# Attention blocks normalised in pairs, their sink columns read from the normalised block

## The chip, the cores and the metric

The kernel runs on one core of one Trainium2 chip. TensorE (PE, with its weight loads as PEld), VectorE (DVE), ScalarE (ACT), GpSimd (POOL) and the DMA queues run side by side and wait for one another by semaphores. The metric is the device time of one execution in microseconds, as the median of several runs.

## What is computed

An attention with sink keys and a sliding window feeds two feed-forward stages. The change touches the attention alone:

```python
keep = is_sink | in_window              # 4 sink keys, window of 128
scores = np.where(keep, scores, -1000000000.0)
scores = scores - np.max(scores, axis=-1, keepdims=True)
a = np.exp(scores)
a = a / (np.sum(a, axis=-1, keepdims=True) + 1e-09)
return np.matmul(a, v).astype(np.float32)
```

Shapes are 2 batches, 8 heads, 768 positions, 64 values per head. Behind it come a soft mixture of 8 experts (8 rounds of normalising the gates) and a gated product of two projections, each multiplied out with an output matrix.

## The kernel before

`fast_attention` works on 8 units (two heads each) of 6 blocks of 128 query rows: G = 48 blocks, block g being block i = g mod 6 of its unit. A block's keys are the 128 of the block before it, 16 sink columns, and its own 128: 272 columns (i = 0 has its own 128 alone). Since the first key block holds the sinks, only blocks with i of 2 or more need the sink columns apart; they are split into a high and a low part (`ak`, three copies of 2 x 16 columns) and multiplied in one fp32r product.

The loop at the end of the function writes one slot for each g, and that is the order of every engine's queue; there is no scheduler behind it (the schedule is manual). In slot g stand, in this order:

1. PE: the transposing of the sink parts of block g - 4 (`turn_sinks`, L851), then `sinks` in two slots of a unit, then the scores of block g (L801), then the products with v (`pv`, L874) of the unit that is six blocks behind.
2. ACT: the exponentials of block g - 1 with their row sums (L819).
3. DVE: `mask_max` of block g (L810: mask, scale and row maximum, for two heads).
4. `normal(g - 1)`: DVE adds the guard to the sums (L827) and takes the reciprocal (L828); POOL multiplies both heads' rows (L831) into `a`, and for i of 2 or more makes the sink parts (L837 the 16 normalised columns, L840 the high part twice, L843 the low part).
5. PE: `turn(g - 4)`, the transposes of that block's `a` (L860, L861), which DVE copies out (L864).
6. ACT: the copy of the sink parts out of PSUM (L852), and in two slots `leave` (L888).
7. One step of `warm`: work for the next stage, spread over the slots. It puts sums (L403, L181, L184, L189, L197) and splits (L162) on POOL, splits on DVE (L162), casts on ACT, and in four of the slots the gates' logits on PE (L293, L301).

Buffers turn: 3 for the exponentials `ex`, the sums `sm` and the maxima `mx`, 4 for `a` and `ak`, 2 for `sw`. Behind the 48 slots come 7 more that drain the attention while the first expert product starts, and then the feed-forward stages (`rest`, L87 above all).

Of the kernel before, what the change touches and what calls it, by code (L numbers as in the profile page):

```python
# [12 lines left out]
FR = mybir.dt.float32r  # L13
# [3 lines left out]
ALU = mybir.AluOpType  # L17
# [6 lines left out]
NB = S // 128  # L24
NSK = 16
KW = 128 + NSK
SW = 128 + KW
# [16 lines left out]
def fused_kernel(  # L44
# [711 lines left out]
    with tc.If(flag > 0) as cond:  # L756
        fast_attention(tc, env)
# [4 lines left out]
def fast_attention(tc, env):  # L762
# [3 lines left out]
    pe, act, dve, pool = nc.tensor, nc.scalar, nc.vector, nc.gpsimd  # L766
# [6 lines left out]
    def open_pool(n, name):  # L773
        return sides[n].enter_context(
            tc.tile_pool(name=name, bufs=1, side=("left", "right")[n], reuse_waits="tile")
        )

    def tiles(pool, name, n, *shape):
        return [pool.tile([128, *shape], F32, name=f"{name}{i}") for i in range(n)]

    last, soon = open_pool(0, "last"), open_pool(1, "soon")
# [1 line left out]
    env["lasting"](last)  # L783
    vs, ast, at = (env[n][0] for n in ("vs", "ast", "at"))
    sos, exs = tiles(soon, "so", 2, 2, SW), tiles(soon, "ex", 3, 2, SW)
    ats, aks, sws = tiles(last, "a", 4, 2, SW), tiles(last, "ak", 4, 3, 2, NSK), tiles(last, "sw", 2, 2, NSK)
    mxs, sms = tiles(last, "mx", 3, 2), tiles(last, "sm", 3, 2)
    G = UN * NB
    warming = env["warm"]()

    raw_s, exps, attn = {}, {}, {}

    def scores(g):
        u, i = divmod(g, NB)
        lo = KW if i == 0 else 0
        ps = [bank[(2 * g + h) % 3] for h in range(2)]
        for h in range(2):
            r = slice(h * 64, (h + 1) * 64)
            kf = kt[u][r].rearrange("p j c -> p (j c)")
            rhs = kf[:, 0:128] if i == 0 else kf[:, (i - 1) * KW:(i - 1) * KW + SW]  # L800
            pe.matmul(  # L801
                out=ps[h][:, lo:SW], lhsT=qt[u][r, i * 128:(i + 1) * 128], rhs=rhs, start=True, stop=True
            )
        mx, so = mxs[g % 3], sos[g % 2]
        raw_s[g] = so, mx, ps, lo

    def mask_max(g):
        so, mx, ps, lo = raw_s[g]
        for h in range(2):
            dve.tensor_tensor_reduce(  # L810
                out=so[:, h, lo:], in0=ps[h][:, lo:SW], in1=mask[:, 2 - min(g % NB, 2), lo:], scale=-0.125,
                scalar=3.0e38, op0=ALU.add, op1=ALU.min, accum_out=mx[:, h:h + 1],
            )

    def exp(g):
        so, mx, _, lo = raw_s.pop(g)
        sm, ex = sms[g % 3], exs[g % 3]
        for h in range(2):
            act.activation(  # L819
                out=ex[:, h, lo:], in_=so[:, h, lo:], func=ACTF.Exp, scale=-1.0, bias=mx[:, h:h + 1],  # L820
                accum_out=sm[:, h:h + 1],
            )
        exps[g] = ex, sm, lo

    def normal(g):
        ex, sm, lo = exps.pop(g)
        dve.tensor_scalar(out=sm, in0=sm, scalar1=1.0e-9, scalar2=None, op0=ALU.add)  # L827
        dve.reciprocal(out=sm, in_=sm)  # L828
        a = ats[g % 4]
        for h in range(2):  # L830
            pool.tensor_scalar(  # L831
                out=a[:, h, lo:], in0=ex[:, h, lo:], scalar1=sm[:, h:h + 1], scalar2=1.0, op0=ALU.mult, op1=ALU.mult
            )
        ak = None
        if g % NB >= 2:
            ak, sw = aks[g % 4], sws[g % 2]
            pool.tensor_tensor(  # L837
                out=sw, in0=ex[:, :, 128:KW], in1=sm.unsqueeze(2).broadcast_to([128, 2, NSK]), op=ALU.mult
            )
            pool.tensor_copy(  # L840
                out=ak[:, 0::2].bitcast(FR), in_=sw.unsqueeze(1).broadcast_to([128, 2, 2, NSK])
            )
            pool.tensor_tensor(out=ak[:, 1], in0=sw, in1=ak[:, 0], op=ALU.subtract)  # L843
        attn[g] = a, ak

    def turn_sinks(g):
        _, ak = attn[g]
        if ak is None:
            return None
        dst = bank[7][0:6 * NSK, 384:512]  # L850
        pe.transpose(out=dst, in_=ak.rearrange("p n h c -> p (n h c)"), identity=ident)  # L851
        return lambda: act.copy(out=ast[0:6 * NSK, g % NB * 128:g % NB * 128 + 128], in_=dst)  # L852

    def turn(g):
        i = g % NB
        a, _ = attn.pop(g)
        ps = bank[3 + g % 2]
        for h in range(2):
            if i:
                pe.transpose(out=ps[:, h * 256:h * 256 + 128], in_=a[:, h, 0:128], identity=ident)  # L860
            pe.transpose(out=ps[:, h * 256 + 128:h * 256 + 256], in_=a[:, h, KW:SW], identity=ident)  # L861
        c0 = 0 if i else 128
        o = i * 256 - 128
        dve.tensor_copy(  # L864
            out=at[:, :, o + c0:o + 256], in_=ps.rearrange("p (h c) -> p h c", h=2)[:, :, c0:256]
        )

    def pv(u, j):
        v = nat[u]
        spans = [(j, min(j + 2, NB))] if j != 2 else [(2, 3), (3, 4)]  # L870
        for a, b in spans:
            c = slice(j * 256 + (a - j) * 128, j * 256 + (b - j) * 128)
            for h in range(2):
                pe.matmul(  # L874
                    out=bank[6 + a // 3][h * 64:(h + 1) * 64, (a % 3) * 128:(a % 3 + b - a) * 128],
                    lhsT=v[:, j, h], rhs=at[:, h, c],
                    start=j == 0 or a == 3 and j == 2, stop=j == 5 or a == 2 and j == 2, skip_group_check=True,
                )

    def sinks(u, half):  # L880
        a, b = (2, 3) if half == 0 else (3, 6)
        dst = bank[6 + half][:, (a % 3) * 128:(a % 3 + b - a) * 128]
        c = slice(a * 128, b * 128)
        pe.matmul(out=dst, lhsT=vs[:, u], rhs=ast[:, c], start=False, stop=False, skip_group_check=True)

    def leave(u, half):
        b, p = divmod(u, H // 2)
        act.copy(out=xt[:, b, p, half * HT:(half + 1) * HT], in_=bank[6 + half][:, 0:HT])  # L888

    LAG_T, LAG_V = 4, 6  # L890
    for g in range(G + LAG_V + 1):
        u, i = divmod(g, NB)
        t = g - LAG_T
        rest = turn_sinks(t) if 0 <= t < G else None
        w, j = divmod(g - LAG_V, NB) if 0 <= g - LAG_V < G else (0, 0)
        if j in (3, 5):
            sinks(w, j // 5)
        if g < G:
            scores(g)
        for n in range(max(j - 1, 0), j + (j == 5)):  # L900
            pv(w, n)
        if 0 <= g - 1 < G:
            exp(g - 1)
        if g < G:
            mask_max(g)
        if g == 0:
            masks()
        if 0 <= g - 1 < G:
            normal(g - 1)
        if 0 <= t < G:  # L910
            turn(t)
        if rest:
            rest()
        if i == 3 and u + 1 < UN:
            copy_sinks(u + 1)
        if j in (3, 5):
            leave(w, j // 5)
        if (g == 1 or i == 5 and u) and u + 2 < UN:
            load_q(sp, u + 2)
            load_k(sp, u + 2)  # L920
            load_v(u + 2)
        if 4 <= g < 8:
            sink_values((g - 4) * (UN // 4))
        if g == G:
            sides[1].close()
            env["take"](open_pool(1, "steps_r"))
        if g in env["WARM"]:
            next(warming)
# [163 lines left out]
```

## Time and profile before

| | |
|---|---|
| median of 3 runs | 1428.04 us (1427.96 to 1428.43) |
| span of the profiled execution | 1426.2 us |
| share of the span, PE / PEld / DVE / ACT / POOL | 99% / 86% / 70% / 41% / 43% |
| DMA, mean | 90 GB/s |

The profile gives the profiled execution by its span, from its first instruction to its last; no other time of that execution is shown, and the median of the runs lies 1.8 us above it, which is what lies around the span. A busy share is an average over the whole span. Matmuls overlap, so a busy PE says little by itself. The attention takes roughly the first 110 us, and there the shares are quite different from the table; the rows below are mostly from that stretch.

### The profile page before, as it was taken

To read this page: it belongs to the slowest core of one execution; us is meant where nothing else is said; L and a number is where in the kernel's file an instruction comes from. 1 tells how busy PE (TensorE), PEld (TensorE's weight loads), DVE (VectorE), ACT (ScalarE), POOL (GpSimd) and SP (SyncE) were. 2 spreads that over 40 slices of the span, in tenths; PEclk is the share of its full clock that TensorE was granted. 3 is DMA by queue.
4 is the path that set the end of the run, shared out by engine and by line. 5 is a ranking of instruction groups with operands and counts; after the bars stand their busy time and mean duration, and the time that the engine had idled before them with its cause. 6 is when DMAs were issued, how large, how long until landed. Compare 5 with 4: busy or idle time off the path is not lost.

```text
span 1426.2 us, 20470 instructions
## 1 busy us (share of the span) xinstructions
PE 1406.6 (99%) x7219; PEld 1229.2 (86%) x7219; DVE 999.8 (70%) x1978; ACT 586.4 (41%) x1327; POOL 607.8 (43%) x729
## 2 busy tenths in 40 slices
PE   8999999999999999999999999999999999999998
PEld 5558889898898998989989889898899888888997
DVE  7986877676776766786766766775665876777763
ACT  5774434333333333443443333333333444444442
POOL 6994434343434343443344433434343434324430
PEclk8999999999999999999999999999999999999999
DMA  6312333233233323322243323332222121223101
GB/s 187 116 49 60 104 104 110 89 111 119 82 111 107 123 89 111 105 73 89 82 127 103 111 89 119 104 90 67 74 59 75 54 73 55 72 66 112 60 30 47
DMA packets 146352, 128.65 MB, mean 90 GB/s; under 512 B 8192, under 2 KB 117120, under 8 KB 146240
## 3 DMA queue, kind: packets, MB, share of 16 engines
q1 hardware_dynamic: 145808, 126.99, 28.8%
q8 instruction: 58, 0.95, 0.3%
q14 instruction: 54, 0.44, 0.1%
q10 hardware_dynamic: 432, 0.26, 0.1%
HBM read 114.38 MB, written 12.58 MB: 89 GB/s over the span
## 4 chain that ended last, share of the span: by engine, by line
PE 90%; DVE 6%; ACT 1%; issue 1%; POOL 1%; DMA 0%; DVEq 0%; POOLq 0%; ACTq 0%
PE bank L87 84%; PE bank L801 2%; PE bank L874 1%; DVE ring L162 1%; DVE flat L162 1%; PE bank L860 1%; DVE hid L162 1%; PE bank L861 1%; ACT hid L530 1%; DVE room L529 1%; DMA small<-in_window 0%; DVE so L810 0%; PE bank L851 0%; PE bank L453 0%; DVE at L864 0%
## 5 line engine op out<-in xcount | busy, mean ns | idle before, releaser
L87 PE MATMUL bank<-flat,ring 128*128 128x384 f32 x3696 | 729.0, 339 | 6.2 <-DVE mid L340 2.6
L87 PE MATMUL bank<-ring,hid 128*128 128x512 f32 x2736 | 710.6, 395 | 0.3 <-ACT hid L530 0.3
L87 PEld LDWEIGHTS bank<-flat,ring 128*128 128x128 f32 x3696 | 657.3, 188 | 53.6 <-ACT acc L457 3.2
L87 PEld LDWEIGHTS bank<-ring,hid 128*128 128x128 f32 x2736 | 506.3, 188 | 83.9 <-DVE hid L162 2.7
L162 POOL TENSOR_TENSOR ring<-raw,ring 128x512 fp32r<-128x512 f32 x152 | 206.3, 1361 | 383.6 <-ACT ring L194 342.2
L324 ACT ACTIVATE hid<-mid 128x384 fp32r<-128x384 f32 x191 | 100.7, 527 | 420.4 <-DVE mid L344 316.7
L181 POOL TENSOR_TENSOR room<-raw 128x256 f32<-128x256 f32 x88 | 91.5, 1040 | 358.5 <-DVE ring L162 291.8
L325 DVE SCALAR_TENSOR_TENSOR hid<-mid,hid 128x384 fp32r<-128x384 f32 x191 | 127.4, 667 | 43.6 <-ACT hid L324 35.4
L162 DVE TENSOR_TENSOR ring<-raw,ring 128x512 fp32r<-128x512 f32 (+1 forms) x176 | 142.1, 808 | 0.2 <-ACT ring L182 0.2
L342 DVE TENSOR_TENSOR mid<-mid,bank 128x384 f32<-128x384 f32 x87 | 48.1, 553 | 111.3 <-PE bank L87 111.0
L162 DVE TENSOR_TENSOR ring<-room,ring 128x512 fp32r<-128x512 f32 x176 | 116.0, 693 | 0.9 <-ACT ring L211 0.9
L336 ACT COPY mid<-bank 128x384 f32<-128x384 f32 x87 | 41.7, 479 | 142.6 <-PE bank L87 142.3
L340 DVE TENSOR_TENSOR mid<-mid,bank 128x384 f32<-128x384 f32 x87 | 48.0, 552 | 74.6 <-PE bank L87 74.6
L197 POOL TENSOR_TENSOR room<-raw,room 128x256 f32<-128x256 f32 x88 | 83.4, 948 | 6.8
L189 POOL TENSOR_TENSOR room<-room,raw 128x256 f32<-128x256 f32 x88 | 76.5, 869 | 0.0
L184 POOL TENSOR_TENSOR room<-raw 128x256 f32<-128x256 f32 x88 | 69.3, 788 | 13.3 <-DVE ring L162 11.5
L344 DVE TENSOR_TENSOR mid<-mid,bank 128x384 f32<-128x384 f32 x88 | 48.7, 553 | 32.7 <-PE bank L87 31.9
L325 DVE SCALAR_TENSOR_TENSOR hid<-bank,hid 128x384 fp32r<-128x384 f32 x64 | 35.4, 553 | 43.6 <-ACT hid L324 43.6
L351 DVE TENSOR_TENSOR mid<-mid,bank 128x384 f32<-128x384 f32 x88 | 48.4, 550 | 21.2 <-PE bank L87 21.0
L324 ACT ACTIVATE hid<-bank 128x384 fp32r<-128x384 f32 x64 | 31.4, 491 | 58.4 <-PE bank L87 57.0
L205 ACT CAST ring<-room 128x512 fp32r<-128x512 f32 x88 | 54.6, 621 | 2.0 <-POOL room L189 2.0
L211 ACT CAST ring<-room 128x512 fp32r<-128x512 f32 x88 | 54.6, 620 | 0.6 <-POOL room L197 0.3
(154 smaller groups left out, 1194.1 us busy)
## 6 DMA issues: line engine op xcount, KB each, us to landing
raw<-in_moe_w SPq DMA_DIRECT2D x256, 256.0 KB, 2.7
raw<-kept SPq DMA_DIRECT2D x72, 256.0 KB, 3.2
kept<-room SPq DMA_DIRECT2D x36, 256.0 KB, 2.9
raw<-in_moe_w_a SPq DMA_DIRECT2D x12, 512.0 KB, 3.8
raw<-in_moe_w_b SPq DMA_DIRECT2D x12, 512.0 KB, 3.8
raw<-in_moe_w_out SPq DMA_DIRECT2D x12, 512.0 KB, 3.7
out_x<-xt SPq DMA_DIRECT2D x11, 256.0 KB, 2.1
qt<-in_q SPq DMA_DIRECT2D x6, 384.0 KB, 3.1
```

What stands on the lines that cost most here:

```text
L87: pe.matmul(out=dst, lhsT=a, rhs=b, start=start and n == 0, stop=stop and n == 2, skip_group_check=not check,)
L162: eng.tensor_tensor(out=lo, in0=src, in1=hi.bitcast(F32), op=ALU.subtract)
L181: pool.tensor_tensor(out=s1, in0=a21, in1=a22, op=ALU.add)
L184: pool.tensor_tensor(out=s3, in0=a11, in1=a21, op=ALU.subtract)
L189: pool.tensor_tensor(out=s2, in0=s1, in1=a11, op=ALU.subtract)
L197: pool.tensor_tensor(out=s4, in0=a12, in1=s2, op=ALU.subtract)
L205: act.copy(out=halves[0][0], in_=halves[0][2])
L211: act.copy(out=halves[1][0], in_=halves[1][2])
L324: act.activation(out=h[:, 0, f, t0], in_=src, func=ACTF.Relu)
L325: later.append(lambda: dve.scalar_tensor_tensor(out=h[:, 1, f, t0], in0=src, scalar=0.0, in1=h[:, 0, f, t0].bitcast(F32), op0=ALU.max, op1 ...
L344: dve.tensor_tensor(out=m[:, 2], in0=m[:, 1], in1=ps, op=ALU.add)
L351: dve.tensor_tensor(out=m[:, 1], in0=m[:, 1], in1=ps, op=ALU.subtract)
```

## The change

`normal` is called in even slots only, and does two blocks, g - 2 and g - 1, at once. The guard and the reciprocal run over both blocks' sums (four columns). POOL then normalises both blocks (four instructions), and, unless the pair is blocks 0 and 1 of a unit, makes the sink parts of both from columns 128 to 144 of the normalised `a`: two copies for the high part, one subtraction for the low part. `sw` is gone; `a`, `ak` and `sm` are one tile each with four places, and `sm` has four places where there were three buffers.

```diff
-    ats, aks, sws = tiles(last, "a", 4, 2, SW), tiles(last, "ak", 4, 3, 2, NSK), tiles(last, "sw", 2, 2, NSK)
-    mxs, sms = tiles(last, "mx", 3, 2), tiles(last, "sm", 3, 2)
+    ats, aks, sms = (tiles(last, x, 1, 4, *n)[0] for x, n in (("a", (2, SW)), ("ak", (3, 2, NSK)), ("sm", (2,))))
+    mxs = tiles(last, "mx", 3, 2)
...
     def normal(g):
-        ex, sm, lo = exps.pop(g)
-        dve.tensor_scalar(out=sm, in0=sm, scalar1=1.0e-9, scalar2=None, op0=ALU.add)
-        dve.reciprocal(out=sm, in_=sm)
-        a = ats[g % 4]
-        for h in range(2):
-            pool.tensor_scalar(
-                out=a[:, h, lo:], in0=ex[:, h, lo:], scalar1=sm[:, h:h + 1], scalar2=1.0, op0=ALU.mult, op1=ALU.mult
-            )
-        ak = None
-        if g % NB >= 2:
-            ak, sw = aks[g % 4], sws[g % 2]
-            pool.tensor_tensor(
-                out=sw, in0=ex[:, :, 128:KW], in1=sm.unsqueeze(2).broadcast_to([128, 2, NSK]), op=ALU.mult
-            )
-            pool.tensor_copy(
-                out=ak[:, 0::2].bitcast(FR), in_=sw.unsqueeze(1).broadcast_to([128, 2, 2, NSK])
-            )
-            pool.tensor_tensor(out=ak[:, 1], in0=sw, in1=ak[:, 0], op=ALU.subtract)
-        attn[g] = a, ak
+        n = slice(g % 4, g % 4 + 2)
+        dve.tensor_scalar(out=sms[:, n], in0=sms[:, n], scalar1=1.0e-9, scalar2=None, op0=ALU.add)
+        dve.reciprocal(out=sms[:, n], in_=sms[:, n])
+        for m in (g, g + 1):
+            ex, sm, lo = exps.pop(m)
+            for h in range(2):
+                pool.tensor_scalar(
+                    out=ats[:, m % 4, h, lo:], in0=ex[:, h, lo:], scalar1=sm[:, h:h + 1], scalar2=1.0,
+                    op0=ALU.mult, op1=ALU.mult,
+                )
+            attn[m] = ats[:, m % 4], aks[:, m % 4] if g % NB else None
+        if g % NB:
+            src = ats[:, n, :, 128:KW]
+            for x in (0, 2):
+                pool.tensor_copy(out=aks[:, n, x].bitcast(FR), in_=src)
+            pool.tensor_tensor(out=aks[:, n, 1], in0=src, in1=aks[:, n, 0], op=ALU.subtract)
...
-        if 0 <= g - 1 < G:
-            normal(g - 1)
+        if g % 2 == 0 and 0 <= g - 2 < G:
+            normal(g - 2)
```

In the changed kernel the normalising stands at L832, the sink parts at L840 and L841, their transposing at L848, the other transposes at L857 and L858, and DVE's copy of them at L861.

How the queues change is seen at three places.

On POOL, in the first unit, blocks 3 and 4 stood like this (`a`, `ak`, `sw`, `ex` and `sm` with the numbers of their buffers; `vs` is a part of the sinks' values that is prepared once):

```order
L831 TENSOR_SCALAR a_232<-ex_226,sm_242 128x272 x2
L837 TENSOR_TENSOR sw_238<-ex_226,sm_242 128x32
L840 CAST ak_236<-sw_238 128x2x32
L843 TENSOR_TENSOR ak_236<-sw_238,ak_236 128x32
L162 TENSOR_TENSOR vs<-raw_75,vs 32x256
L831 TENSOR_SCALAR a_229<-ex_227,sm_243 128x272 x2
L837 TENSOR_TENSOR sw_237<-ex_227,sm_243 128x32
L840 CAST ak_233<-sw_237 128x2x32
L843 TENSOR_TENSOR ak_233<-sw_237,ak_233 128x32
```

Now blocks 2 and 3, and after them 4 and 5, stand like this:

```order
L832 TENSOR_SCALAR a_229<-ex_228,sm_231 128x272 x2
L832 TENSOR_SCALAR a_229<-ex_226,sm_231 128x272 x2
L840 CAST ak_230<-a_229 128x2x32 x2
L841 TENSOR_TENSOR ak_230<-a_229,ak_230 128x2x32
L162 TENSOR_TENSOR vs<-raw_75,vs 32x256 x2
L832 TENSOR_SCALAR a_229<-ex_227,sm_231 128x272 x2
L832 TENSOR_SCALAR a_229<-ex_228,sm_231 128x272 x2
L840 CAST ak_230<-a_229 128x2x32 x2
L841 TENSOR_TENSOR ak_230<-a_229,ak_230 128x2x32
```

Four instructions of normalising and three small ones now stand in a row for a pair, where each block had two and three; the sink parts of a pair's first block come behind the normalising of its second.

On DVE, slots 3 and 4 stood like this (`so` is the masked block, `mx` its maxima; what an instruction waits for is in brackets):

```order
L810 ISA so_225,mx_239<-bank_63,mid 128x272 [waits PE_49]
L810 ISA mx_239 128x1
L810 ISA so_225,mx_239<-bank_64,mid 128x272 [waits PE_49]
L810 ISA mx_239 128x1
L827 TENSOR_SCALAR sm_244<-sm_244 128x2 [waits Activation_49]
L828 RECIPROCAL sm_244<-sm_244 128x2 [waits DVE_49]
L810 ISA so_224,mx_240<-bank_65,mid 128x272 [waits PE_49]
L810 ISA mx_240 128x1
L810 ISA so_224,mx_240<-bank_63,mid 128x272 [waits PE_49]
L810 ISA mx_240 128x1
L827 TENSOR_SCALAR sm_242<-sm_242 128x2 [waits Activation_49]
L828 RECIPROCAL sm_242<-sm_242 128x2 [waits DVE_49]
```

Now they stand like this:

```order
L810 ISA so_225,mx_232<-bank_63,mid 128x272 [waits PE_49]
L810 ISA mx_232 128x1
L810 ISA so_225,mx_232<-bank_64,mid 128x272 [waits PE_49]
L810 ISA mx_232 128x1
L810 ISA so_224,mx_233<-bank_65,mid 128x272 [waits PE_49,Activation_49]
L810 ISA mx_233 128x1
L810 ISA so_224,mx_233<-bank_63,mid 128x272 [waits PE_49,Activation_49]
L810 ISA mx_233 128x1
L827 TENSOR_SCALAR sm_231<-sm_231 128x4 [waits Activation_49]
L828 RECIPROCAL sm_231<-sm_231 128x4 [waits DVE_49]
```

The sums of block 2, which stood ahead of the masking of block 4, now stand behind it, together with those of block 3.

On PE, from the head of slot 6 to the head of slot 7, before:

```order
L851 MATMUL bank_70<-ident,ak_235 96x128 [waits Pool_49]
L801 MATMUL bank_63<-xt 128x128 [waits DMAHW7_49,DMAHW0_49,DVE_49]
L801 MATMUL bank_64<-xt 128x128 [waits DVE_49]
L860 MATMUL bank_66<-ident,a_231 128x128
L861 MATMUL bank_66<-ident,a_231 128x128
L860 MATMUL bank_66<-ident,a_231 128x128
L861 MATMUL bank_66<-ident,a_231 128x128
L851 MATMUL bank_70<-ident,ak_236 96x128 [waits Activation_49,Pool_49]
L801 MATMUL bank_65<-xt 128x272 [waits DVE_49]
```

And now:

```order
L848 MATMUL bank_70<-ident,ak_230 96x128 [waits Pool_49]
L801 MATMUL bank_63<-xt 128x128 [waits DMAHW7_49,DMAHW0_49,DVE_49]
L801 MATMUL bank_64<-xt 128x128 [waits DVE_49]
L857 MATMUL bank_66<-ident,a_229 128x128
L858 MATMUL bank_66<-ident,a_229 128x128
L857 MATMUL bank_66<-ident,a_229 128x128
L858 MATMUL bank_66<-ident,a_229 128x128
L848 MATMUL bank_70<-ident,ak_230 96x128 [waits Activation_49]
L801 MATMUL bank_65<-xt 128x272 [waits DVE_49]
```

PE's order is the same, and a slot still opens with the sink parts of the block four behind; only the wait for POOL is now at the pair's first block alone (slot 6), and the second (slot 7) has none of its own.

## Rows read from the trace of the kernel before

**Rows 1.** The page, chain that ended last: shares of the span by line.

```profile
PE bank L87 84%; PE bank L801 2%; PE bank L874 1%; DVE ring L162 1%; DVE flat L162 1%; PE bank L860 1%; DVE hid L162 1%; PE bank L861 1%; ACT hid L530 1%; DVE room L529 1%; DMA small<-in_window 0%; DVE so L810 0%; PE bank L851 0%; PE bank L453 0%; DVE at L864 0%
```

**Rows 2.** Windows, 50 to 60 us: length; busy us (instructions) by engine; granted clock; DMA.

```profile
50.00:60.00 10.00, 9.72 (x63) 5.21 (x63) 9.69 (x41) 8.50 (x32) 9.01 (x25) 1.00 0.45 143
```

**Rows 3.** Timeline of PE, heads of slots: start, length in us; engine, line; [idle before].

```profile
19.26 0.80 PE L801 MATMUL bank<-xt 64*128 64x128 f32 x4
...
53.20 0.73 PE L801 MATMUL bank<-kt,qt 64*128 64x272 f32 x4
...
55.62 0.49 PE L801 MATMUL bank<-kt,qt 64*128 64x128 f32 x4
...
58.72 0.73 PE L801 MATMUL bank<-kt,qt 64*128 64x272 f32 x4
...
62.55 1.10 PE L801 MATMUL bank<-kt,qt 64*128 64x272 f32 x4
...
76.13 0.73 PE L801 MATMUL bank<-kt,qt 64*128 64x272 f32 x4
...
77.92 0.73 PE L801 MATMUL bank<-kt,qt 64*128 64x272 f32 x4
...
79.97 0.83 PE L293 MATMUL bank<-xt,gate 128*8 128x384 f32 x8
...
81.89 0.73 PE L301 MATMUL bank<-mid 128*128 128x8 f32 x6
...
105.69 0.29 PE L851 MATMUL bank<-ident,ak 128*96 128x128 f32 x1
```

**Rows 4.** Groups by line, first 200 us: count | busy us, mean ns | idle before, releasers.

```profile
L831 POOL TENSOR_SCALAR a<-ex,sm 128x272 f32<-128x272 f32 (+1 forms) x96 | 45.2, 483 | 3.8 <-ACT ex L819 1.4 <-DVE sm L828 0.7 <-ACT xt L888 0.7
...
L827 DVE TENSOR_SCALAR sm<-sm 128x2 f32<-128x2 f32 x48 | 12.0, 250 | 0.9 <-POOL ak L840 0.5 <-ACT ex L819 0.4
...
L837 POOL TENSOR_TENSOR sw<-ex,sm 128x32 f32<-128x32 f32 x32 | 9.2, 288 | 0.0
L843 POOL TENSOR_TENSOR ak<-sw,ak 128x32 f32<-128x32 f32 x32 | 9.2, 287 | 2.6
...
L840 POOL CAST ak<-sw 128x64 fp32r<-128x64 f32 x32 | 8.6, 270 | 2.1
...
L403 POOL TENSOR_TENSOR acc<-xt 128x384 f32<-128x384 f32 x4 | 4.0, 1000 | 0.0
```

**Rows 5.** Timeline of DVE, three places where it waited for the scores.

```profile
14.40 0.17 DVE L828 RECIPROCAL sm<-sm 128x2 f32<-128x2 f32 x1
...
16.84 0.17 DVE L828 RECIPROCAL sm<-sm 128x2 f32<-128x2 f32 x1
...
75.06 0.44 DVE L810 CUSTOM_DVE_ANT_0 so<-bank,mid 128x272 f32<-128x272 f32 x1 [0.26 <-PE bank L801]
...
75.98 0.17 DVE L828 RECIPROCAL sm<-sm 128x2 f32<-128x2 f32 x1
...
81.50 0.29 DVE L810 CUSTOM_DVE_ANT_0 so<-bank,mid 128x128 f32<-128x128 f32 x1 [0.73 <-PE bank L801]
```

**Rows 6.** Timeline of PE, the scores and sink transposes that belong to these.

```profile
18.91 0.42 PE L851 MATMUL bank<-ident,ak 128*96 128x128 f32 x1
...
74.30 0.73 PE L801 MATMUL bank<-kt,qt 64*128 64x272 f32 x4
...
80.73 0.32 PE L851 MATMUL bank<-ident,ak 128*96 128x128 f32 x1
80.97 0.49 PE L801 MATMUL bank<-kt,qt 64*128 64x128 f32 x4
...
87.93 0.31 PE L851 MATMUL bank<-ident,ak 128*96 128x128 f32 x1 [0.89 <-POOL ak L843]
```

**Rows 7.** Timeline of POOL: one start behind DVE, one end that PE waited for.

```profile
14.74 1.99 POOL L831 TENSOR_SCALAR a<-ex,sm 128x272 f32<-128x272 f32 x4 [0.72 <-DVE sm L828]
...
87.63 0.25 POOL L843 TENSOR_TENSOR ak<-sw,ak 128x32 f32<-128x32 f32 x1
```

More of the change, by code (lines that the diff above doesn't have):

```diff
@@ L816, in exp @@
         so, mx, _, lo = raw_s.pop(g)
-        sm, ex = sms[g % 3], exs[g % 3]
+        sm, ex = sms[:, g % 4], exs[g % 3]
         for h in range(2):
```

## The prediction

> **What bounds the kernel now.** I read the page's chain first. 84% of the span hangs on PE's L87, the products of the feed-forward stages [rows 1], which the change does not touch; what the change can move lies in the attention, and comes through one for one, because the stages behind start when PE leaves it. Then the windows: in a typical stretch DVE is busy 9.69 of 10 us, POOL 9.01, PE 9.72, at the full granted clock of 1.00 (2.4 GHz) [rows 2]. Three engines are near full, so the shares do not tell which one sets the pace. The timeline of PE does. The interval from one block's scores to the next is a slot. From the scores of block 6 at 19.26 to the head of slot 48 at 105.69 [rows 3] PE needs 86.43 us for seven units, 12.35 us each.
>
> PE's own need is read from stretches where no wait is seen. Blocks 0 and 1 of a unit take 58.72 - 55.62 = 3.10 us, blocks 2 and 3 take 62.55 - 58.72 = 3.83, block 4 takes 77.92 - 76.13 = 1.79 and block 5 takes 55.62 - 53.20 = 2.42, together 4.21 [rows 3]. That is 11.14 us for a unit. Two units also hold gate logits twice, 0.76 us (79.97 to 80.73) and 0.73 [rows 3, 6], 3.0 us in all. So PE needs 7 x 11.14 + 3.0 - 0.24 (the last head has no scores behind its L851) = 80.7 of the 86.43. **Waiting inside the attention is worth 5.7 us, and no more than that can be won there.**
>
> **What is removed.** 24 of 48 pairs of L827 and L828 leave DVE: 24 x (0.250 + 0.17) = 10 us [rows 4, 5]. On POOL 32 x (0.288 + 0.270 + 0.287) = 27.0 us of sink parts become 16 x 3 instructions; at the same means 13.5 us, so some 13 us less [rows 4]. Both are busy time on engines that lie beside PE. They pay only where one of them makes PE wait, at most those 5.7 us.
>
> The Trainium skill, in "Perfetto Trace Analysis", section "Optimizing Scalar/DVE Operations", says that grouping and larger operations can improve throughput where the engine is saturated, and that splitting can finish work sooner where an engine is not saturated but makes others wait. By the first half the sum would be the gain of 5.7 us alone (the first rival below), by the second it would be a loss. DVE's 9.69 of 10 speaks for the first half; the path below, for the second.
>
> **What is moved, and who waits.** PE opens slot t + 4 with the sink parts of block t, ahead of the scores of block t + 4 in its queue. Before, block t was normalised behind the masking of block t + 1: three slots lay between. Now a pair's first block is normalised behind the masking of block t + 2, behind its partner's four multiplications, and its sink parts last of all: two slots remain, for a longer piece of work. The path, from the scores of an even block g (blocks 4, or 0, of a unit) to those of block g + 2:
>
> - scores to masking: 75.06 - 74.30 = 0.76 us for 272 columns; 81.50 - 80.97 = 0.53 for 128 [rows 5, 6]. Both rows show DVE waiting for PE.
> - masking of two heads, guard and reciprocal: 75.98 + 0.17 - 75.06 = 1.09 us [rows 5]. For 128 columns each head's instruction is 0.15 shorter (0.29 against 0.44), so 0.79. I cost four columns of sums like two.
> - DVE to POOL: 14.74 - (14.40 + 0.17) = 0.17 us [rows 5, 7].
> - POOL, the pair: 4 x 0.483 = 1.93 us, then three small instructions. At the means of the three that they replace they take 0.85; with 0.1 for the gap before an instruction that waits for the one ahead and for the wider subtraction (64 columns, where the nearest row has 32) I take 2.9 us in all. Bounds: 2.6, if the copies overlap and each takes the 0.25 of the POOL row [rows 4, 7], and 3.3, if each of the three runs 0.13 over its mean.
> - POOL to PE and the transposing: 87.93 - (87.63 + 0.25) = 0.05, then 80.97 - 80.73 = 0.24 us [rows 6, 7].
>
> The sum is 0.76 + 1.09 + 0.17 + 2.9 + 0.29 = **5.21 us** behind block 4, where PE has work for 4.21; and 0.53 + 0.79 + 0.17 + 2.9 + 0.29 = **4.68 us** behind block 0, where it has 3.10. Behind block 2 nothing changes: its pair (blocks 0 and 1) has no sink parts, and its `a` is wanted only at the transposes late in slot 4; I take PE's 3.83. A unit then takes 5.21 + 4.68 + 3.83 = 13.72 us. The logits (0.76, 0.73) lie in these waits and cost nothing more: 4.21 + 0.76 and 3.10 + 0.73 are below 5.21 and 4.68.
>
> **The sum.** Seven units: 7 x 13.72 - 0.24 = 95.8 us against 86.43, **+9.4**. In the first unit the reciprocal of slot 4 ends at 17.01; 0.17 + 2.9 + 0.05 later, at 20.13, PE can take the sink parts of block 2, which it took at 18.91 [rows 5, 6]: **+1.2**. Together +10.6 us on the profiled span of 1426.2; the median lies 1.8 above that span, so 1428.04 + 10.6 = **1438.6 us**.
>
> Edits that I cost at nothing: the copies of sink keys (L668) move ahead of POOL's pair in its queue and are wanted two slots later. The three buffers of exponentials are read a slot later than before, but POOL is done with the first of a pair some 3 us into slot t + 2, and it is overwritten in slot t + 4. DVE's new waits for ACT ahead of the masking are for exponentials a slot old. POOL's steps of `warm` (L403, 1.0 us each [rows 4]) come behind the pair's work and fit in what a pair leaves free, 5.21 - 2.9 = 2.3 us; without that cover each costs its own length. The queues of the DMAs are not moved.
>
> **Rivals.**
>
> *The relief wins (faster).* DVE and POOL are freed by 10 and 13 us, the backlog that makes PE wait goes, and the pair's sink parts come in time. All 5.7 us would be won: 1422.3. It decides at 3.10 and 4.21 us: the paths behind blocks 0 and 4 have to be shorter than that. For it: the idle time before L851 at 87.93 is 0.89 us, with POOL as releaser [rows 6], and POOL is what gets lighter. Against it: behind block 0 the lead to POOL (0.53 + 0.79 + 0.17) and the four multiplications (1.93) already make 3.42. It is the result that the Trainium skill's rule on grouping ("Perfetto Trace Analysis") would give. Chance 0.06.
>
> *They cancel (no change).* The two paths together would have to be 8.5 us and not 9.9, so that 7 x (8.5 + 3.83) is about 86.4: POOL's pair in 2.2 us. Its four multiplications leave 0.27 of that for three instructions of a quarter microsecond each. 1428. Chance 0.07.
>
> *POOL's other work falls into the path.* Where two or three steps of `warm` stand in a row ahead of a pair, they exceed the free 2.3 us. If all eight L403 came on the path at 1.0 us, 1446.6; DVE's splits ahead of the masking of block 4 could add a few tenths in some units. Chance 0.08.
>
> *The merged tile is waited for as a whole.* If PE's transposes waited for the newest write to `a`, every even slot would pay the path to POOL's multiplications, tens of microseconds. The order shows no POOL wait at those transposes in slot 6. Chance 0.01.
>
> **How the numbers follow.** The forecast has 0.78. The bounds of the pair's work, 2.6 and 3.3, make 15 passes (two in each of seven units, one in the first) x (-0.3 to +0.4) = -4.5 to +6 us: 1434 to 1444.6. For 8 in 10 I reach a little towards the neighbours: 1432 to 1446, leaving out the faster and the equal case and the top of the third. About 0.2%, 2.9 us, is what a measurement of this kernel can tell from no change. Slower by more: 0.78 + 0.08 + 0.01 = 0.87; within: 0.07; faster: 0.06.
>
> **What would show it.** In the profile after, L848 at the heads of even slots waits for POOL's L841, about 1 us behind block 4 and 1.6 behind block 0, in every unit; odd slots do not wait. A unit takes 13.7 us from block 0 to block 0, 3.8 of it from block 2 to block 4. POOL and DVE are busy less of each 10 us than before, and POOL's idle time ends on DVE's L828. If the units stay near 12.3 us or below, the path is shorter than I made it, and the four multiplications or the masking is the term to look at. If waits show ahead of blocks 2 or at DVE, something other than the pair is late. A granted clock below 1.00 behind these waits would also break the sum.

## The result, and the profile after

The changed kernel takes 1444.45 us (median of 4 runs, 1441.93 to 1446.98) against 1428.13 for the kernel before (1427.96 to 1428.43): a ratio of 1.0114, 95% interval 1.0101 to 1.0126. It is slower, as forecast, and inside the range, but by more than the forecast: the profiled execution took 1444.98 with a span of 1443.2, so 17.0 us more span than before, where the sum said 10.6.

PE's timeline, the scores at the heads of blocks 0 of the units (blocks 6, 12, 18, ...), one stretch within a unit, and the head of slot 48 (start, length in us; engine, line; [idle before]):

```profile
20.35 0.80 PE L801 MATMUL bank<-xt 64*128 64x128 f32 x4
...
34.19 0.49 PE L801 MATMUL bank<-kt,qt 64*128 64x128 f32 x4
...
48.56 0.49 PE L801 MATMUL bank<-kt,qt 64*128 64x128 f32 x4
...
53.48 0.73 PE L801 MATMUL bank<-kt,qt 64*128 64x272 f32 x4
...
58.83 0.73 PE L801 MATMUL bank<-kt,qt 64*128 64x272 f32 x4
...
64.19 0.49 PE L801 MATMUL bank<-kt,qt 64*128 64x128 f32 x4
...
68.52 0.31 PE L848 MATMUL bank<-ident,ak 128*96 128x128 f32 x1 [1.32 <-POOL ak L841]
68.77 0.73 PE L801 MATMUL bank<-kt,qt 64*128 64x272 f32 x4
...
122.83 0.31 PE L848 MATMUL bank<-ident,ak 128*96 128x128 f32 x1 [0.97 <-POOL ak L841]
```

These answer to [rows 3]. Block 6 starts 1.09 us later (20.35 against 19.26), and the seven units from there to slot 48 take 122.83 - 20.35 = 102.48 us against 86.43, **+16.05**. The two make 17.1, so the stages behind the attention add nothing. Split by the stretches of the prediction, all seven units:

| stretch of a unit | predicted | measured | in us |
|---|---|---|---|
| blocks 0 to 2 | 4.68 | mean 4.87 (4.58 to 5.05) | +1.3 |
| blocks 2 to 4 | 3.83 | 3.83 five times, 5.35 twice | +3.0 |
| block 4 to the next block 0 | 5.21 | mean 5.54 (5.11 to 5.93) | +2.3 |

The last column is what the stretch cost beyond the prediction over all units; together 6.6. The miss is 6.4 (17.0 - 10.6), since the first unit came 0.1 us below its term and the stages behind the attention took 0.1 less than before.

The list of waits, 12 to 125 us (engine, line, releaser: us in total, times, longest). PE and its weight loads show largely the same gaps, so the two rows are not added:

```profile
PEld bank L848 <- POOL ak L841: 22.0, 15, 2.0
DVE so L810 <- PE bank L801: 17.6, 19, 1.9
POOL a L832 <- ACT ex L819: 17.5, 10, 3.4
PE bank L848 <- POOL ak L841: 16.4, 13, 1.8
...
POOL a L832 <- DVE sm L828: 11.9, 7, 3.3
```

Fifteen waits at the sink parts' transposing stand in this stretch, one for each pair with sink parts but the last, whose transposing falls into the drain (slot 50). All other engines now wait too: DVE for PE's scores, POOL for DVE's reciprocal. The list puts 17.5 us of POOL's waiting down to ACT, because ACT's event came last by the profile; but in all fourteen pairs with sink parts that the seven units wait for, the multiplications start 0.19 to 0.20 us behind the end of L828, and the exponentials that end just then are a later block's. Groups by line, first 200 us, answering to [rows 4]:

```profile
L832 POOL TENSOR_SCALAR a<-ex,sm 128x272 f32<-128x272 f32 (+1 forms) x96 | 47.4, 512 | 35.9 <-ACT ex L819 17.5 <-DVE sm L828 11.9 <-PE bank L881 2.5
...
L840 POOL CAST ak<-a 128x64 fp32r<-128x64 f32 x32 | 7.7, 272 | 1.0
L841 POOL TENSOR_TENSOR ak<-a,ak 128x64 f32<-128x64 f32 x16 | 5.1, 319 | 0.0
L827 DVE TENSOR_SCALAR sm<-sm 128x4 f32<-128x4 f32 x24 | 5.1, 212 | 0.3 <-ACT ex L819 0.3
```

POOL's sink parts fell from 27.0 us to 12.8 and DVE's L827 from 12.0 to 5.1, as costed. POOL's idle time ahead of the multiplications rose from 3.8 us to 35.9: the relief is there and turned into waiting.

Windows, answering to [rows 2] (length; busy us (instructions) of PE, PEld, DVE, ACT, POOL; granted clock; DMA). First ten us, then two single ones inside them:

```profile
50.00:60.00 10.00, 8.34 (x51) 4.52 (x47) 6.71 (x21) 5.68 (x22) 6.71 (x14) 0.83 0.03 13
...
52.00:53.00 1.00, 0.00 (x0) 0.00 (x0) 0.80 (x2) 0.14 (x2) 0.94 (x4) 1.00 0.00 0
...
56.00:57.00 1.00, 1.00 (x5) 0.48 (x4) 1.00 (x2) 0.00 (x0) 1.00 (x3) 0.50 0.00 0
```

DVE is busy 6.71 where it was 9.69, POOL 6.71 where it was 9.01. And something the forecast had only named as a way to break: PE stands still for the whole microsecond from 52 to 53, and in the three from 55 to 58 its granted clock is 0.50, the lower level of 1.2 GHz. That is one of the two stretches of 5.35 us (53.48 to 58.83); the other is 112.61 to 117.96, behind a wait of the same kind.

### The profile page after: what moved, and what is told of

Read it like the earlier page. It is cut to its first block, busy times and chain, and to the rows that moved or that the text cites. A ratio compares the mean times of both kernels' runs of the same rounds, so it can differ in the third digit from the quotient of the medians.

```text
span 1443.2 us, 20364 instructions
## 1 busy us (share of the span) xinstructions
PE 1408.3 (98%) x7219; PEld 1228.7 (85%) x7219; DVE 993.0 (69%) x1930; ACT 587.8 (41%) x1327; POOL 597.6 (41%) x681
## 4 chain that ended last, share of the span: by engine, by line
PE 88%; DVE 6%; POOL 2%; ACT 2%; issue 1%; DMA 0%; DVEq 0%; POOLq 0%; ACTq 0%
PE bank L87 83%; PE bank L801 2%; POOL a L832 1%; PE bank L871 1%; DVE ring L162 1%; DVE flat L162 1%; DVE hid L162 1%; ACT hid L530 1%; PE bank L857 1%; ACT ex L819 1%; DVE room L529 0%; PE bank L858 0%; PE bank L848 0%; POOL ak L840 0%; DMA small<-in_window 0%
## 5 line engine op out<-in xcount | busy, mean ns | idle before, releaser
L184 POOL TENSOR_TENSOR room<-raw 128x256 f32<-128x256 f32 x88 | 69.0, 784 | 12.7 <-DVE ring L162 10.8
L832 POOL TENSOR_SCALAR a<-ex,sm 128x272 f32<-128x272 f32 (+1 forms) x96 | 47.4, 512 | 35.9 <-ACT ex L819 17.5
L819 ACT ACTIVATE ex<-so,mx 128x272 f32<-128x272 f32 (+1 forms) x96 | 47.4, 495 | 20.6 <-DVE mx L810 16.6
L205 ACT CAST ring<-room 128x512 fp32r<-128x512 f32 x88 | 54.7, 621 | 2.6 <-POOL room L189 2.6
```

Of the source, the lines that this page charges most:

```text
L184: pool.tensor_tensor(out=s3, in0=a11, in1=a21, op=ALU.subtract)
L205: act.copy(out=halves[0][0], in_=halves[0][2])
L819: act.activation(out=ex[:, h, lo:], in_=so[:, h, lo:], func=ACTF.Exp, scale=-1.0, bias=mx[:, h:h + 1], accum_out=sm[:, h:h + 1],)
L832: pool.tensor_scalar(out=ats[:, m % 4, h, lo:], in0=ex[:, h, lo:], scalar1=sm[:, h:h + 1], scalar2=1.0, op0=ALU.mult, op1=ALU.mult,)
```

## The experiments

Theory: the pair's path (scores, masking, reciprocal, four multiplications, sink parts, transposing) sets the pace because it has only two slots; what exceeds the sum is DVE's work beside POOL's, and the clock. Rival: the relief is real and worth something, and another part of the change (the wider tiles, reading the sinks from `a`) costs the time.

**1. Reading the sinks from the normalised block, one block at a time.** The kernel before, with this part of the change alone:

```diff
-            ak, sw = aks[g % 4], sws[g % 2]
-            pool.tensor_tensor(
-                out=sw, in0=ex[:, :, 128:KW], in1=sm.unsqueeze(2).broadcast_to([128, 2, NSK]), op=ALU.mult
-            )
+            ak = aks[g % 4]
+            src = a[:, :, 128:KW]
...
```

> The kernel before, with one part of the change alone: each block by itself, in its own slot, its sink parts read from the normalised block (two small instructions for three). Theory: no block comes later, GpSimd has 32 x 0.29 = 9 us less to do, and some of the 5 us of waits for it go: 1423 to 1428 us. Rival (reading the normalised block is what costs): slower than 1429.

Measured: 1428.85 us, ratio 1.0003 (0.9993 to 1.0013): no change. POOL is freed of 9 us of L837, though the multiplications' mean rises from 483 to 525 ns, which takes 4 us of it back. PE's weight loads of the sink parts wait 2.7 us in all for POOL (0.6 put down to the last of the sink parts, 2.1 to the multiplications) where they waited 3.8, yet no time is won. This part is neither the cost nor a gain, and POOL's relief alone buys nothing.

**2. A slot more for the pair.** The changed kernel with the transposes five slots behind the scores; their PE part stands ahead of the normalising, DVE's copy behind it:

```diff
-        dve.tensor_copy(
+        return lambda: dve.tensor_copy(
...
-    LAG_T, LAG_V = 4, 6
+    LAG_T, LAG_V = 5, 6
...
+        turned = turn(t) if 0 <= t < G else None
         if g % 2 == 0 and 0 <= g - 2 < G:
             normal(g - 2)
-        if 0 <= t < G:
-            turn(t)
+        if turned:
+            turned()
```

In this kernel the sink parts of a unit's last block are transposed into a PSUM bank in which its second half is being summed, so the sums of that half come out different; the instructions are the same ones.

> The changed kernel, with the transposing of sink parts and blocks on TensorE one slot later (lag 5 for 4). Theory (the pair's sink parts come too late for the head of the even slot): three slots lie between again, the waits at the heads of even slots shrink from 0.8 to 1.8 us to under 0.3, no half-clock stretches behind them, 1423 to 1430 us. Its own risk: the products with v now need what VectorE copied out one slot before, so they may wait for it. Rival (the pair's work itself, or the merged tiles, cost the time): 1438 or more.

Measured: 1430.94 us (1.0020, 1.0011 to 1.0030), 13.5 us below the changed kernel. The waits of PE's weight loads at L848 for POOL fall from 22.0 us to 2.1, and the clock stays at 1.00 from 30 us on. What is late next is the copy of `at`: it was a slot ahead of the products with v that read it, and now stands right in front of them. From the list of waits:

```profile
PEld bank L871 <- DVE at L861: 15.6, 31, 1.0
```

**3. The same slot for single blocks.** The kernel before with the same edit, and the same part of the sums affected.

> The control to the lag of 5: the kernel before, one block at a time, with the same later transposing. Theory (the lag costs what the products with v wait for VectorE's copies, whatever the normalising does): 1429 to 1433 us, the same waits at the products. Rival (the pairing still costs something at lag 5): 1425 to 1428, clearly below the 1430.9 of the pair at lag 5.

Measured: 1434.38 us (1.0044, 1.0028 to 1.0061), with 21.8 us of waits for the copy where the pairs had 15.6. With equal lags the pairs are 3.4 us ahead (the two intervals just touch, but no run of either lies among those of the other), so pairing as such is not what costs. This went against both expectations for single blocks, which had not seen that the copy would be waited for more.

**4. Sink parts right behind each block's own multiplications.** Same pairs, POOL's order changed:

```diff
-        if g % NB:
-            src = ats[:, n, :, 128:KW]
-            for x in (0, 2):
-                pool.tensor_copy(out=aks[:, n, x].bitcast(FR), in_=src)
-            pool.tensor_tensor(out=aks[:, n, 1], in0=src, in1=aks[:, n, 0], op=ALU.subtract)
+            if g % NB:
+                src = ats[:, m % 4, :, 128:KW]
+                for x in (0, 2):
+                    pool.tensor_copy(out=aks[:, m % 4, x].bitcast(FR), in_=src)
+                pool.tensor_tensor(out=aks[:, m % 4, 1], in0=src, in1=aks[:, m % 4, 0], op=ALU.subtract)
```

> The changed kernel, but each block's sink parts made right behind its own multiplications: six small instructions for a pair where there are three. Theory: the first block's sink parts are ready about 0.95 us earlier, the waits behind blocks 4 and 0 fall by about that, and with them the half-clock stretches; 1428 to 1434 us although GpSimd works some 12 us more. Rival (the amount of GpSimd's work sets the time): 1444 or slower.

Measured: 1430.83 us (1.0017, 1.0007 to 1.0027). POOL now issues six small instructions for a pair instead of three, and its sink parts take 12.7 + 8.0 = 20.7 us instead of 12.8. The kernel is 13.6 us faster all the same, since the first block's sinks no longer stand behind the partner's two multiplications. Its row of waits at L848, against the 22.0 above:

```profile
PEld bank L848 <- POOL ak L841: 8.3, 16, 1.0
```

This is the second half of the rule that the prediction drew from the Trainium skill ("Perfetto Trace Analysis", section "Optimizing Scalar/DVE Operations"): where ScalarE or VectorE is not saturated but makes other engines wait, smaller pieces may let work be completed sooner. Here the engine is GpSimd, and the trace agrees: 7.9 us more POOL work, 13.6 us less time, because the pieces let the first block's part go ahead of its partner's multiplications.

**5. The pair's sums ahead of the next masking.** `normal(g - 2)` called before `mask_max(g)`:

```diff
+        if g % 2 == 0 and 0 <= g - 2 < G:
+            normal(g - 2)
         if g < G:
             mask_max(g)
...
-        if g % 2 == 0 and 0 <= g - 2 < G:
-            normal(g - 2)
```

> The changed kernel, with the pair's guard, reciprocal and normalising written ahead of the masking of block g in the even slot. Theory: GpSimd starts the pair when the exponentials of its second block are done, about 1 us earlier, so the waits fall by about 1 us each; the masking comes 0.4 us later. 1428 to 1435 us. Rival (the pair is late through GpSimd's own queue, not through the masking ahead of it): 1441 to 1447.

Measured: 1437.36 us (1.0067, 1.0050 to 1.0084), a miss: 7 us won and not 10 to 16. The masking's 1.1 us leave the path, but DVE comes to the sums before ACT's row sums of the slot before are there, and the masking queues behind that:

```profile
PEld bank L848 <- POOL ak L841: 11.9, 14, 1.7
...
DVE sm L827 <- ACT ex L819: 7.7, 16, 1.7
```

**6. Both of these edits.**

> Sinks first and normalising ahead of the masking together. Theory (the two shortenings of the path add): the waits for sink parts at the heads of even slots, 8 us in all with sinks first alone, nearly vanish, 1425 to 1429 us. Rival (the masking that is now behind the normalising comes late, and TensorE waits for VectorE in place of GpSimd): 1431 or more.

Measured: 1430.73 us (1.0020, 1.0011 to 1.0030): no better than the fourth alone. It stands just below the rival's 1431, and the list of waits points the rival's way: no wait for POOL's L841 is left near the top, DVE waits for ACT, and PE's weight loads wait 4.5 us for the masking where the fourth's wait 3.3. That is 1.2 us more against the 8.3 that went, and block 6 stands at 20.05 where the fourth has it at 19.32; where the rest of the gain is lost was not shown.

```profile
DVE sm L827 <- ACT ex L819: 9.0, 16, 1.7
...
PEld bank L801 <- DVE mx L810: 4.5, 9, 1.2
```

**7. DVE's splits at another place.** In `warm`, the step that loads parts and makes splits was moved by one slot: `g % 3 == 2` for `g % 3 == 1`.

> The changed kernel with the weight pair's preparation (its casts, splits and sums) one slot later, in blocks 2 and 5 for 1 and 4. Theory (VectorE's splits in block 4's slots hold up GpSimd's multiplications, which take 2.1 to 2.4 us there and 1.9 elsewhere): they take 1.9 us behind block 4 too, the stretch from block 4 to the next block 0 falls from 5.5 to about 5.1 us, and the time by 2 to 3 us. Rival (the length there is not due to the splits): the stretches and the time stay.

Measured: 1445.59 us (1443.33 to 1448.2; ratio 1.0118, 1.0101 to 1.0135): no gain. The trace shows why the mechanism holds and the time does not follow. The changed kernel, POOL's four multiplications of three pairs, and DVE's split beside the first two:

```profile
45.11 2.40 POOL L832 TENSOR_SCALAR a<-ex,sm 128x272 f32<-128x272 f32 x4 [1.79 <-ACT ex L819]
...
61.00 2.13 POOL L832 TENSOR_SCALAR a<-ex,sm 128x272 f32<-128x272 f32 x4 [3.31 <-DVE sm L828]
63.20 0.41 POOL L840 CAST ak<-a 128x64 fp32r<-128x64 f32 x2
63.57 0.32 POOL L841 TENSOR_TENSOR ak<-a,ak 128x64 f32<-128x64 f32 x1
65.82 1.89 POOL L832 TENSOR_SCALAR a<-ex,sm 128x272 f32<-128x272 f32 x4 [1.93 <-ACT ex L819]
```

```profile
45.14 0.69 DVE L162 TENSOR_TENSOR ring<-raw,ring 128x512 fp32r<-128x512 f32 x1
...
61.03 0.42 DVE L162 TENSOR_TENSOR ring<-raw,ring 128x256 fp32r<-128x256 f32 x1
```

With the splits moved, the same pairs (POOL's timeline of this kernel):

```profile
47.89 1.89 POOL L832 TENSOR_SCALAR a<-ex,sm 128x272 f32<-128x272 f32 x4 [2.40 <-ACT ex L819]
...
61.76 1.90 POOL L832 TENSOR_SCALAR a<-ex,sm 128x272 f32<-128x272 f32 x4 [1.10 <-ACT ex L819]
```

Without a split beside them the multiplications take 1.89 us, with one 2.13 to 2.40, and the two stretches from block 4 to block 0 fell from 5.62 and 5.36 to 5.13 and 5.12. But the same stretches in the units with gate logits grew (5.98 and 6.48 for 5.86 and 5.77); ahead of the second, POOL's pair started at 90.93, straight behind an L403, 0.9 us after the end of L828 and not 0.2. The granted clock fell in four of the windows of 10 us between 40 and 120 us (0.83, 0.77, 0.89 and 0.66) instead of two, and the first full unit took 15.01 us instead of 13.84, since the clock rose later there too. That ate the gain in the profiled execution, which is the longest of the four.

**8. PE kept at work behind the waits' heads.** Five products of constants, whose result nobody reads, at the end of the slots of blocks 1 and 5:

```diff
+        if 6 < g < G and i in (1, 5):
+            for _ in range(5):
+                pe.matmul(out=bank[2][:, 384:512], lhsT=env["ones"], rhs=env["ones"], start=True, stop=True)
```

> The changed kernel with five extra products of constants on TensorE at the end of the slots of blocks 1 and 5, where it then waits for the pair (their results are used by nothing; about 1 us, inside waits of 0.8 to 1.8 us). Theory (the half-clock stretches seen at 54 and 113 us are a consequence of the waits): the granted clock stays 1.00 from 30 us to the end of the attention, blocks 2 and 3 always take 3.83 us, the runs lie closer together; 1440 to 1443 us. Rival (the clock falls for another reason): windows at 0.83 remain and the time is 1442 to 1448.

Measured: 1446.13 us (1445.88 to 1446.58; 1.0128, 1.0111 to 1.0145), not faster. All stretches from block 2 to block 4 are 3.83 and the clock is 1.00 from 30 us on. But in three units the filling itself was longer than the wait that it filled: blocks 0 to 2 took 6.08, 6.04 and 5.63 us where they had taken 4.89, 4.86 and 4.88.

**9. The same only where it does not get in the way**, `(12 < g < 29 or 37 < g < G)` in place of `6 < g < G`.

> The changed kernel with five products of constants, which nobody reads, at the end of the slots of blocks 1 and 5 as in the earlier run, but only in the units that hold no gate logits and not in the first two units, where the earlier run's filling itself made the stretches from block 0 to block 2 longer (6.08, 6.04 and 5.63 us against 4.9). Theory: the two stretches of 5.35 us (blocks 2 to 4, where the granted clock fell to the lower level behind a wait) are 3.83 again, and nothing else changes: 3.0 us below the changed kernel's profiled execution, a median of 1440.5 to 1442.5, and runs within 1.5 us of one another. Rival: the fall of the clock is not caused by the waits, or its cost lies beside the pair's path anyway: 1443.5 us or more.

Measured: 1443.24 us (1443.01 to 1443.63; 1.0104, 1.0088 to 1.0120), an interval that overlaps the changed kernel's; the profiled span is 1441.5, 1.7 less than the changed kernel's. The theory's mechanism is there, its size is not: stretches of 3.83 throughout, the former 5.35 among them (54.56 to 58.39), and windows at full clock:

```profile
50.00:60.00 10.00, 9.46 (x73) 5.90 (x69) 7.72 (x31) 6.52 (x24) 6.71 (x14) 1.00 0.17 58
110.00:120.00 10.00, 9.32 (x73) 5.90 (x72) 6.81 (x26) 5.50 (x21) 5.29 (x13) 1.00 0.00 0
```

That gives the 3.0 us back in this execution. 1.1 of them were lost in the first full unit, ahead of the edit: there the clock rose only after 26 us in this execution, and at 24 in the changed kernel's, and that unit took 14.93 us instead of 13.84. The runs lie 0.6 us apart instead of 5.

**10. A slot more for the products with v too.** Experiments 2 and 3 with lags five and seven, for pairs and for single blocks. As run, the load of a unit's v stood ahead of the last products of the unit whose buffer it takes, so these products read another unit's values.

> The changed kernel with the transposes five slots behind the scores (the turn's PE part ahead of the normalising, DVE's copy behind it) and the products with v seven behind, so that one whole slot again lies between a block's copy out of PSUM and the products that read it. Theory: pairing costs nothing in itself, it only needs one slot more; with the transposes alone moved (1430.94) PE waited 15.6 us in front of the products with v for DVE's copy of the slot before, and those waits now go. Then PE has no wait left but a few tenths a unit, up to 5.7 us of waiting can be won against the kernel before, and the drain behind slot 47 pays about 0.5: 1423 to 1427 us, L871 without a wait for DVE above 4 us in all. Rival: DVE itself is the limit once PE does not wait for the pair (its masking comes late for the exponentials, the splits stand ahead of it), so that the waits only move, to L801 or L857: 1428 to 1431 us.

> The kernel before (one block at a time) with the same lags, five and seven. It tells what the slot alone brings from what pairing brings. Theory: with a slot more nobody waits for POOL's sink parts, but POOL is still busy 9 of 10 us and DVE more than 9, so that less of the 5.7 us is won than with pairs: 1425 to 1429 us, 1 to 4 us above the paired kernel with these lags (at lags five and six the single blocks stood 3.4 us above the pairs). Rival: the slot alone brings all, and pairing nothing: equal to the paired one within 1 us.

Measured: 1448.39 us (1.0143, 1.0127 to 1.0160) for pairs, 1449.92 (1.0155, 1.0141 to 1.0170) for single blocks. Neither says anything on its question: PE waited for the loads' transfers in three units of each, here in the pairs' timeline:

```profile
59.55 1.36 PE L871 MATMUL bank<-at,natv 128*64 128x256 f32 x8 [4.51 <-DMA natv<-in_v]
```

**11. The pairs again, with that load a slot later:**

```diff
-            load_v(u + 2)
+        if (g == 1 or i == 0 and u > 1) and u + 1 < UN:
+            load_v(u + 1 + (g == 1))
```

> The paired kernel with lags five and seven once more, now with the load of a unit's values of v one slot later (the slot of block 0, behind the last products of the unit whose buffer it takes). In the run before it the load still stood in the slot of block 5, ahead of those products, so that they waited for the load's transfer (24 us of waiting in three places, up to 4.7 us each) and read the wrong unit's values. Two units of that run hold no such wait: from block 0 to block 0 they take 43.11 - 31.63 = 11.48 and 54.55 - 43.11 = 11.44 us, against 12.35 before. Theory: all units now take that; the unit bound to PE's own work is 11.14. Seven units 80.5 to 82 us against 86.4, the drain one slot longer (up to 1.5 us): 1422.5 to 1426 us. Rival: in the units with DVE's splits or gate logits the waits return, as in the run with the transposes alone moved: 1427 us or more.

Measured: 1427.98 us, ratio 0.9996 (0.9986 to 1.0005): the kernel before, within what can be told. The gain inside the attention is there. PE's timeline, scores of block 6, of block 47, and a product of the first expert behind the attention:

```profile
18.01 0.80 PE L801 MATMUL bank<-xt 64*128 64x128 f32 x4
...
100.94 0.73 PE L801 MATMUL bank<-kt,qt 64*128 64x272 f32 x4
...
122.45 1.29 PE L87 MATMUL bank<-flat,ring 128*128 128x384 f32 x6
```

In the kernel before the same three stand at:

```profile
103.47 0.73 PE L801 MATMUL bank<-kt,qt 64*128 64x272 f32 x4
...
122.80 1.28 PE L87 MATMUL bank<-flat,ring 128*128 128x384 f32 x6
```

with block 6 at 19.26 [rows 3]. PE is 2.5 us ahead at block 47 and 0.35 ahead at the product: the drain, one slot longer, takes 2.2 back. PE is busy 9.65 to 10.00 us in each 10 of the attention. Two units take 11.49 and 11.41 us from block 0 to block 0, four 12.26 to 13.00, among them the two with gate logits. So the rival's time came, by a mixture: waits return in part, and most of what is won goes in the drain. No version tried beats the kernel before. Single blocks with these lags and the load mended were not tried, so whether pairing itself gains anything there stays open.

## Why the prediction was right, and where its sum was short

The path behind block 0 of the unit at 64.19, where nothing runs beside it (DVE's timeline, then POOL's):

```profile
64.82 0.29 DVE L810 CUSTOM_DVE_ANT_0 so<-bank,mid 128x128 f32<-128x128 f32 x1 [1.36 <-PE bank L801]
...
65.45 0.18 DVE L828 RECIPROCAL sm<-sm 128x4 f32<-128x4 f32 x1
...
65.82 1.89 POOL L832 TENSOR_SCALAR a<-ex,sm 128x272 f32<-128x272 f32 x4 [1.93 <-ACT ex L819]
67.78 0.41 POOL L840 CAST ak<-a 128x64 fp32r<-128x64 f32 x2
68.15 0.32 POOL L841 TENSOR_TENSOR ak<-a,ak 128x64 f32<-128x64 f32 x1
```

The kernel before, first 200 us, POOL's multiplications of the larger shape by themselves:

```profile
L831 POOL TENSOR_SCALAR a<-ex,sm 128x272 f32<-128x272 f32 x80 | 39.1, 502 | 2.3 <-DVE sm L828 0.7 <-ACT xt L888 0.7 <-PE bank L801 0.4
```

- **The bound and the path: right.** PE's timeline, not the busy shares, told the pace. L848 at even slots waits for POOL's L841, 0.79 to 1.78 us behind block 4 (about 1 forecast) and 0.99 to 1.79 behind block 0 (1.6), but for the first full unit: there PE still ran at the lower clock, its own work filled the time behind block 0, and only its weight load waited, for 0.17 us. Odd slots do not wait; block 6 stands at 20.35 (20.46 worked out), and a pair without sink parts leaves blocks 2 to 4 at 3.83 where the clock holds. Experiment 2 gives the path its third slot back and 13.5 of the 16.3 us go; experiment 4 shortens it and 13.6 go.
- **The terms, where nothing runs beside them: a little too long.** Behind block 0 of the unit at 64.19: masking starts at 64.82 (0.63 for 0.53), POOL at 65.82, the pair ends at 68.15 + 0.32 = 68.47, so 2.65 us (2.9 taken, bounds 2.6 to 3.3), and the scores follow at 68.77: 4.58 for 4.68. Behind block 4 without a split, experiment 7 shows 5.12 for 5.21.
- **The step that failed: "POOL, the pair: 4 x 0.483 = 1.93 us".** The term is right alone (1.89) and wrong beside DVE's splits, which stand next to it in most units. They lengthen it by 0.24 to 0.51 us in seven of the fourteen paths, and the casts behind it by 0.33 to 0.47 in three more. The 0.483 is also a mean over two shapes: the 128x272 instructions alone took 0.502 before, which makes 2.01 for four. DVE's own small instructions ahead of the pair suffer too: L827 took 0.41 us in place of 0.17 at 74.31, while POOL ran an L403, and 0.44 at 88.75. The prediction put this under a rival as "a few tenths in some units", for the place ahead of the masking, where it happened once (0.3 us, behind the split at 102.34); it is a few tenths in most, beside the multiplications. The paths' means lie 0.42 and 0.29 us above the free values, 5.0 us over seven units, most of it such overlaps and 0.3 of it the lower clock in the first unit; the free values are 1.3 below the sum. Net +3.7.
- **The clock: named, not priced.** The text said that a granted clock below 1.00 behind the waits would break the sum. It cost 2 x (5.35 - 3.83) = 3.0 us in this execution. Experiments 8 and 9 show that the waits are the cause: with PE at work during them the clock holds, and the stretches are 3.83, in one profiled execution of each. Which waits are followed by a fall stays open (last section).
- Together 10.6 + 3.7 + 3.0 = 17.3 against 17.0.
- **The range: held, in part by luck.** Its top came from the bounds of the pair's work, with the clock at nothing. The overlaps and the clock filled it nearly to the end, and one of the four runs, 1446.98, lies above 1446.
- **The relief: no gain on the kernel before, as said.** Experiment 1 takes load from POOL without lateness and gains nothing; experiment 11 gives the pairs a slot more throughout and ends at the kernel before: of its 2.5 us inside the attention the drain takes 2.2 back.
- **Other rivals.** POOL's own steps of `warm` did not fall into the path of the changed kernel: ahead of each of the fourteen pairs POOL stands idle for 0.44 us or more. In experiment 7 one did, with 0.7 us. The transposes wait for POOL's multiplications no more than before (their weight loads 2.1 us in all from 12 to 125 us, 2.2 before), so the merged tile is not waited for as a whole.

## What to carry to other kernels

Before grouping the work of two steps, count the slots between the first of the two and whoever waits for it: grouping takes one slot from it and puts its partner's work in front, and that can cost more than the instructions saved, however busy the engine looks. When a path becomes the bound, price its terms with the neighbours that will run beside them, not from a mean. If the grouping is wanted, move the consumer by a slot in the same edit, and look at what is then late next (the copy, the products, the loads into shared buffers, the drain).

## What the runs showed of the hardware

- **Waits of under two microseconds can cost PE's clock.** In the changed kernel both falls came behind the second of two waits at L848 in a row: 1.48 us (48.32) and 1.66 (53.23), and 1.78 (107.31) and 1.79 (112.36). Some 3 us at a granted clock of 0.50 followed each time, and then the full clock. Pairs of 0.97 and 1.66 (33.95 and 38.86), of 1.21 and 1.32 and of 0.86 and 1.01 were not followed by a fall. The lengths alone do not decide it. In experiment 7 PE's timeline has the same two waits twice, 0.98 and 1.66 with a fall behind them (the scores' four products take 0.96 us), 0.97 and 1.66 without one (0.73); and there the clock also fell behind a first wait, 1.57 us at 93.95, with 10 us since the wait before it. What decides is open.

```profile
35.20 0.31 PE L848 MATMUL bank<-ident,ak 128*96 128x128 f32 x1 [0.98 <-ACT ex L819]
...
40.12 0.31 PE L848 MATMUL bank<-ident,ak 128*96 128x128 f32 x1 [1.66 <-POOL ak L841]
40.36 0.96 PE L801 MATMUL bank<-kt,qt 64*128 64x272 f32 x4
...
50.59 0.31 PE L848 MATMUL bank<-ident,ak 128*96 128x128 f32 x1 [0.97 <-POOL ak L841]
...
55.51 0.31 PE L848 MATMUL bank<-ident,ak 128*96 128x128 f32 x1 [1.66 <-POOL ak L841]
55.76 0.73 PE L801 MATMUL bank<-kt,qt 64*128 64x272 f32 x4
```

- **The clock's rise at the start of the attention moves.** It came at 22 us before the change, at 24 in the changed kernel and after 26 in experiment 9, though PE was busy the same 9.1 of the 12 us from 8 to 20 in the last two; what sets that is open.
- **DVE and POOL slow each other.** Beside a split on DVE (two inputs) POOL's four multiplications lose 0.24 us (split of 0.42), 0.30 (0.60) and 0.51 (0.69); DVE's four-column sum grows from 0.17 to 0.41 beside POOL's L403. The Trainium skill, "SBUF — State Buffer", section "SBUF: two separate sides", says that the two engines share a pair of ports, which an instruction of GpSimd, or one of VectorE with two inputs in SBUF, holds for its whole length while the other is blocked. The trace agrees in kind: POOL loses half to three quarters of the split's length, not all of it.
